# Two changes of order in a fused attention and feed-forward kernel: M's last quarter on ScalarE, and a sum on TensorE

## Chip, core and metric

The kernel runs on one core of a Trainium2 chip. The metric is the device time of one execution in microseconds (us). Engines are named as in the profile: PE is TensorE (PEld its weight loads), ACT is ScalarE, DVE is VectorE, POOL is GpSimd, and SP is SyncE, which here only issues DMAs. Each engine works through its own instructions in the order in which they were issued to it; engines wait for each other by semaphores.

## What is computed

A two-sided cross attention between tokens and a small state, and then a feed-forward product with a leaky ReLU over both results:

```python
scores = scale * x @ state.T            # x: (8, 8, 512, 64), state: (8, 8, 32, 64)
a = softmax(scores)                     # over the 32 state rows
xread = a @ state
a2 = softmax(scale * state @ x.T)       # over the 512 tokens
sread = a2 @ x
x = concat([xread, sread]) as (8 * 544, 512)
h = x @ w_in                            # (512, 2048)
out = maximum(0.01 * h, h) @ w_out      # (2048, 512)
```

Inputs and output are float32; the products run in bfloat16 with float32 sums.

## The kernel before

**Tiling.** The work goes batch by batch (b = 0 to 7). The eight heads and 32 state rows of a batch make two groups of 128 rows, so a score tile is 128 x 2 x 512. Instead of multiplying a by state and the result by w_in, the kernel forms **M** = state times w_in once per batch (`a_m`, L364), 2 x 128 rows by 2048 columns, in four quarters of 512 columns. A quarter is 8 small matmuls into PSUM, then a copy into the SBUF tile `M` (`m_evict`, L384, or copies written out). The hidden layer is then h = M.T times aT (`ff1`, L394, the class `Quad` for batch 0), a leaky ReLU on ACT, and the second product with w_out (`piece`, and from batch 1 on the class `Batch`).

**Order.** The order of all five engines is written by hand (`tc.manual_schedule`): each engine gets its instructions in the order of the calls in the source. A call such as `a_m` issues only to PE, `m_evict(.., SCA)` only to ACT, `cast_x(.., POO)` only to POOL, and the DMA calls to the queue named in them. So a line moved in the source changes the order on an engine only against lines that use the same engine.

**PSUM.** The tiles are named by tag: "sc" and "big" are one buffer of two banks each, "ph" and "py" two buffers of one bank each. A new tile of a tag waits until the old one's last reader is done.

**Batch 0 (L911 to L938).** It is done in two halves u of 256 tokens. `scores0`, `max0`, `split0`, `spread0` put score minus maximum into PSUM; `exp0(u)` (ACT, L850) makes `e10[u]`; `sum0(u)` (PE, L861, four small matmuls `r<-ones,e`) sums it; `recip0(u)` (DVE, L869) takes the reciprocal `q`; `recip0_rows` (PE, L826, `qb<-ident,q`) spreads it over rows; `probs0(u)` (DVE, L877) multiplies into `aT`. Woven into that are M's first quarter (L923), batch 1's first quarter `pm1` (L933) and M's second quarter (L934, tile "big", copied by ACT at L938 in two halves). After it come the ff products of batch 0, eight `Quad`s of four column blocks and one half of the tokens each; the first reads M's first quarter, the second, on columns 512 to 1023, M's second.

**Batches 0, 1 and 2 (L1006 to L1047).** While PE does the second product of batch 0 in pieces (`piece`, L608), batch 1 goes through its softmax: `a_scores(a1)` writes "sc" (L216), `a_shift` (DVE, L226 to L239), `a_max2` (DVE, L288, L290), `a_exp(a1)` (ACT, L246), `a_probs(a1)` (DVE, L251 to L264, the tile `aT`), and `a_exp2(a1, g)` (ACT, L296, with a read of the accumulator each), the exponentials of the other softmax, which are the last readers of the bank "sc". Batch 1's M quarters 1 to 3 go through "ph" and are copied by ACT in two copies of 128 x 512 each (L388). For batch 2 the input `xl`, loaded by a DMA on POOL's queue (L107, issued from L911), is cast to bfloat16: four heads by ACT (L1033, one instruction of 128 x 1024, L113) and four by POOL (L1035); then SP issues the DMA transpose that makes batch 2's `xT` (L1037, L200), and after it the load of batch 3's x (L1043, L107). The pieces of L1039 and the product of M's last quarter (L1040) stand behind these casts in the source. Then PE goes on with the pieces of L1047, and opens batch 2 with `pm = a_m(a2, 0, "sc")`, which takes the bank "sc", and `ff(0)`, which reads batch 1's `aT`.

**From batch 2 on** a loop over the batches repeats one weave of ff products, second products (L679), softmax steps and casts.

Of the kernel before, what the change touches and what calls it, by code (L numbers as in the profile page):

```python
# [30 lines left out]
def kernel(  # L31
# [25 lines left out]
    VEC, SCA, POO = nc.vector.tensor_copy, nc.scalar.copy, nc.gpsimd.tensor_copy  # L57
# [54 lines left out]
    def cast_x(b, h0, h1, copy):  # L112
        copy(  # L113
            xs[b][:, :, h0:h1].rearrange("p t h d -> p h t d"),
            xl[b][:, h0:h1].rearrange("p h (t d) -> p h t d", t=NT),
        )
# [68 lines left out]
    def state_t(i):  # L185
        POO(stb[i][:], stf[i][:])
        nc.sync.dma_start_transpose(st_t[i][:], stb[i][:].rearrange("p b q -> p (b q)"))
# [11 lines left out]
    def a_xt_dma(a):  # L199
        nc.sync.dma_start_transpose(  # L200
            a.xT[:].rearrange("p t k q -> p (t k) q"),
            a.xb[:].rearrange("p t h d -> p (t h d)"),
        )

    def st_of(a, g, k):
        rows = slice(D * g, D * (g + 1))
        if a.b == 0:
            return stbd[rows, k, g ^ (k // 2), :]
        t = st1 if a.b == 1 else st_t[0][:, a.b - 2] if a.b < 4 else st_t[1][:, a.b - 4]
        return t[rows, NS * k:NS * (k + 1)]  # L210
# [153 lines left out]
    def a_m(a, c, tag):  # L364
        if a.M is None:
            a.M = mpool.tile([P, 2, DFF], BF16, name="M", tag="M")
        if tag in ("ph", "py", "phpy"):
            pm = [psum.tile([P, DM], FP32, name="pm", tag=t) for t in (tag[:2], tag[-2:])]
            at = [t[:] for t in pm]
        else:  # L370
            pm = psum.tile([P, 2, DM], FP32, name="pm", tag=tag, bufs=1)
            at = [pm[:, g, :] for g in range(2)]
        for k in range(NK):
            for g in range(2):
                v, r = (k // 2, 2 * (k % 2) + (g ^ (k // 2))) if a.b == 0 else (g, k)
                nc.tensor.matmul(  # L376
                    at[v][NS * r:NS * (r + 1)],
                    lhsT=st_of(a, g, k),
                    rhs=w_in_bf[D * g:D * (g + 1), k, DM * c:DM * (c + 1)],
                    start=True, stop=True,  # L380
                )
        return pm

    def m_evict(a, c, pm, copy):  # L384
        cols = slice(DM * c, DM * (c + 1))
        if isinstance(pm, list):
            for g in range(2):
                copy(a.M[:, g, cols], pm[g][:])  # L388
        else:
            copy(a.M[:, :, cols], pm[:])  # L390
# [211 lines left out]
    def piece(b, hT, i, jq, bank=None, copy=SCA, part=range(4)):  # L602
        if jq == 0:
            y = ys[b, i] = Y()
            y.py = psum.tile([P, DM], FP32, name="py", tag="py")[:] if bank is None else bank
        y = ys[b, i]
        for j in (4 * jq + v for v in part):
            nc.tensor.matmul(  # L608
                y.py, lhsT=hT[:, j, P * i:P * (i + 1)], rhs=w_out_bf[:, j, :],
                start=(j == 0), stop=(j == 15),  # L610
            )
        if jq == 3 and copy is not None:
            y_store(b, i, copy)

    def y_store(b, i, copy):
        tag, bufs = (f"yo{i - 2}", 1) if (b, i) in ((0, 2), (0, 3)) else ("ysb", 3)
        ysb = ypool.tile([P, DM], FP32, name="ysb", tag=tag, bufs=bufs)
        copy(ysb[:], ys[b, i].py)
        if b == B:
            for bb in range(4):  # L620
                r0 = (4 * i + bb) * SROW + S
                nc.sync.dma_start(out[r0:r0 + NS, :], ysb[NS * bb:NS * (bb + 1), :])
        else:
            nc.sync.dma_start(rows_of(b)[i], ysb[:])
# [13 lines left out]
    def weights_sum(dst, m0=0, m1=NM, eng=None):  # L638
        u, v, op = (
            (B12, B11, ALU.subtract), (B11, tw[2], ALU.subtract),  # L640
            (B22, B12, ALU.add), (tw[1], B21, ALU.add),
        )[dst]
        with nc.allow_low_precision(reason="operands of a product"):
            ms = slice(m0, m1)
            (eng or nc.vector).tensor_tensor(out=tw[dst][:, ms], in0=u[:, ms], in1=v[:, ms], op=op)
# [122 lines left out]
    a0, a1, a2 = att_of[:3]  # L768
# [88 lines left out]
    def sum0(u):  # L857
        for v in range(2):
            for q in range(2):
                n = H * v + NK * q  # L860
                nc.tensor.matmul(  # L861
                    r0[u][:, n:n + NK], lhsT=e10[u][:, q, P * v:P * (v + 1)], rhs=ones4[:],
                    start=False, stop=(v == q == 1),
                )

    def recip0(u):
        q = att.tile([P, NG], BF16, name="q0", tag="q0")
        with nc.allow_low_precision(reason="one rounding, of the finished reciprocal"):
            nc.vector.reciprocal(q[:], r0[u][:])  # L869
        return q  # L870
# [52 lines left out]
    pm = a_m(a0, 0, "big")  # L923
# [7 lines left out]
    VEC(a0.M[:, 1, :DM], pm[:, 1, :])  # L931
    probs0(0)
    pm1 = a_m(a1, 0, "sc")  # L933
    pm = a_m(a0, 1, "big")  # L934
    sum0(1)
    q = recip0(1)
    for g in range(2):
        SCA(a0.M[:, g, DM:2 * DM], pm[:, g, :])  # L938

    h0 = hpool.tile([P, 16, S], BF16, name="hT", tag="hT")  # L940
# [42 lines left out]
    for u, j, tag in (  # L983
# [7 lines left out]
        if (u, j) == (0, 8):  # L991
            pm = a_m(a0, 3, "big")
# [37 lines left out]
    weights_sum(2, 0, 4, nc.gpsimd)  # L1030
    weights_sum(1, 0, 4, nc.gpsimd)
    state_t(0)
    cast_x(2, 0, 4, SCA)  # L1033
    for h in range(NK, H):
        cast_x(2, h, h + 1, POO)  # L1035
    a_open(a2, 2)
    a_xt_dma(a2)  # L1037
    for i in (2, 3):
        piece(0, h0, i, 1)  # L1039
    m_evict(a1, 3, a_m(a1, 3, "ph"), SCA)  # L1040
    for g in range(2):
        a_exp2(a1, g)
    load_x(3, nc.sync)  # L1043
# [26 lines left out]
    pm = a_m(a2, 0, "sc")  # L1070
# [42 lines left out]
    pm = [a_m(a2, 1, "big"), a_m(a2, 2, "sc")]  # L1113
# [222 lines left out]
```

## Time and profile before

| | us |
|---|---|
| median of 3 runs | 201.9 |
| lowest, highest | 201.85, 202.06 |
| the profiled execution | 202.15 |
| its span, first to last instruction | 200.4 |
| busy: DVE | 160.4 |
| busy: ACT | 143.6 |
| busy: POOL | 55.5 |

The span lies inside the execution's time; the rest is around it. A row of the timeline gives the start in us from the span's beginning, the length of a group of like instructions in us, the engine, the source line, the operation, the tiles written and read, the shape and the count; in brackets stands how long the engine was idle before and what ended that. A row of waits gives who waited for what: us in total, times, longest. A row of the chain gives start, length and what. A DMA row of the timeline is the issue alone; "us to landing" is in the view of DMA issues.

### The profile page before, as it was taken

To read this page: it belongs to the slowest core of one execution; us is meant where nothing else is said; L and a number is where in the kernel's file an instruction comes from. 1 tells how busy PE (TensorE), PEld (TensorE's weight loads), DVE (VectorE), ACT (ScalarE), POOL (GpSimd) and SP (SyncE) were. 2 spreads that over 40 slices of the span, in tenths; PEclk is the share of its full clock that TensorE was granted. 3 is DMA by queue.
4 is the path that set the end of the run, shared out by engine and by line. 5 is a ranking of instruction groups with operands and counts; after the bars stand their busy time and mean duration, and the time that the engine had idled before them with its cause. 6 is when DMAs were issued, how large, how long until landed. Compare 5 with 4: busy or idle time off the path is not lost.

```text
span 200.4 us, 4995 instructions
## 1 busy us (share of the span) xinstructions
PE 194.9 (97%) x2066; PEld 134.6 (67%) x2066; DVE 160.4 (80%) x249; ACT 143.6 (72%) x263; POOL 55.5 (28%) x82
## 2 busy tenths in 40 slices
PE   7999999999999999999999999999999999999993
PEld 2566634346676767766776677666767788799882
DVE  2576689999999989975997499779978977995622
ACT  3388747599877867978697859787878768767710
POOL 8393174690036005200420040100020024004250
PEclk9999999999999999999999999999999999999999
DMA  6999997999672892559424844290025102310035
GB/s 184 229 207 261 241 294 130 225 292 202 143 192 53 248 264 50 98 206 258 96 39 169 270 55 89 105 164 0 0 108 157 29 0 87 125 56 0 0 95 170
DMA packets 39510, 28.01 MB, mean 140 GB/s; under 512 B 25344, under 2 KB 36736, under 8 KB 39488
## 3 DMA queue, kind: packets, MB, share of 16 engines
q1 hardware_dynamic: 33712, 20.35, 39.6%
q0 software_dynamic: 4944, 6.55, 16.0%
q10 hardware_dynamic: 832, 0.79, 1.4%
q8 instruction: 16, 0.26, 0.5%
q14 instruction: 6, 0.05, 0.1%
HBM read 17.30 MB, written 8.91 MB: 131 GB/s over the span
## 4 chain that ended last, share of the span: by engine, by line
PE 80%; DMA 14%; POOL 2%; ACT 2%; issue 0%; DVE 0%; POOLq 0%
PE yq L679 43%; PE ph L397 22%; DMA xl<-in_x_dram 8%; DMA w_in_bf<-in_moe_w_in_dram 5%; PE pf L475 3%; PE pm L376 3%; PE yu L679 3%; PE pl L564 2%; PE psn L342 1%; PE sc L216 1%; PE py L608 1%; PE phw L410 1%; POOL w_in_bf L126 1%; ACT e L296 1%; ACT xb L113 1%; ACT M L388 0%
## 5 line engine op out<-in xcount | busy, mean ns | idle before, releaser
L403 ACT ACTIVATE hT<-ph 128x512 bf16<-128x512 f32 x100 | 58.5, 605 | 17.8 <-PE ph L397 17.3
L397 PE MATMUL ph<-aT,M 128*128 128x512 bf16 x200 | 57.7, 379 | 0.0
L679 PEld LDWEIGHTS <-su 128*128 128x128 bf16 x480 | 45.9, 98 | 14.8 <-DVE su L668 0.8
L679 PEld LDWEIGHTS <-hT 128*128 128x128 bf16 x336 | 32.3, 98 | 14.3 <-issue 2.5
L679 PE MATMUL yq<-tw_xf,su 128*128 128x256 bf16 x224 | 31.5, 273 | 0.0
L679 PE MATMUL yq<-w_out_bf,hT 128*128 128x256 bf16 x224 | 31.0, 273 | 0.0
L113 POOL CAST xb<-xl 128x512 bf16<-128x512 f32 (+1 forms) x24 | 13.8, 614 | 48.4 <-DMA xl<-in_x_dram 48.4
L668 DVE TENSOR_TENSOR su<-hT 128x1024 bf16<-128x1024 bf16 (+1 forms) x27 | 18.9, 703 | 6.7 <-ACT hT L403 6.7
L397 PEld LDWEIGHTS <-M 128*128 128x128 bf16 x200 | 19.5, 98 | 5.7 <-issue 0.2
L751 POOL TENSOR_TENSOR yo<-sv,sv 128x512 f32<-128x512 f32 x7 | 9.2, 1310 | 41.0 <-issue 20.3
L688 ACT COPY sv<-yq 128x512 f32<-128x512 f32 x28 | 16.3, 585 | 3.0 <-PE yq L679 2.5
L679 PE MATMUL yq<-tw_x,su 128*128 128x256 bf16 x112 | 15.5, 273 | 0.0
L679 PE MATMUL yq<-w_out_bf,su 128*128 128x256 bf16 x112 | 15.3, 273 | 0.0
L691 DVE TENSOR_TENSOR yo<-yq,sv 128x512 f32<-128x512 f32 x20 | 13.6, 682 | 1.5 <-PE yq L679 1.5
L679 PE MATMUL yq<-tw_x,hT 128*128 128x256 bf16 x104 | 14.5, 273 | 0.0
L390 ACT CAST M<-pm 128x1024 bf16<-128x1024 f32 x12 | 12.2, 1019 | 0.2 <-PE pm L376 0.2
L296 ACT ACTIVATE e<-sc,mcols 128x512 bf16<-128x512 f32 x16 | 11.0, 694 | 0.6 <-DVE mcols L290 0.6
L608 PEld LDWEIGHTS <-hT 128*128 128x128 bf16 x64 | 5.8, 98 | 7.0 <-issue 1.1
L668 DVE TENSOR_TENSOR su<-su,hT 128x1024 bf16<-128x1024 bf16 x14 | 9.7, 692 | 0.5
L288 DVE TENSOR_REDUCE mcol<-sc 128x2 f32<-128x1024 f32 x8 | 9.7, 1215 | 0.0
L668 DVE TENSOR_TENSOR su<-hT,su 128x2048 bf16<-128x2048 bf16 (+1 forms) x8 | 9.2, 1155 | 0.0
L226 DVE TRANSPOSE_TENSOR_REDUCE mrow<-sc 128x32 f32<-128x1024 f32 x7 | 8.7, 1242 | 0.5 <-PE sc L216 0.5
(173 smaller groups left out, 303.7 us busy)
## 6 DMA issues: line engine op xcount, KB each, us to landing
out_dram<-yo SPq DMA_DIRECT2D x12, 512.0 KB, 2.8
xl<-in_x_dram SPq DMA_DIRECT2D x5, 1024.0 KB, 6.7
w_in_bf<-in_moe_w_in_dram POOLq DMA_DIRECT2D x4, 512.0 KB, 7.8
w_out_bf<-in_moe_w_out_dram POOLq DMA_DIRECT2D x2, 512.0 KB, 12.6
x<-in_x_dram POOLq DMA_DIRECT2D x2, 512.0 KB, 11.5
w_out_bf<-in_moe_w_out_dram POOLq DMA_DIRECT2D x4, 256.0 KB, 13.7
xl<-in_x_dram POOLq DMA_DIRECT2D x1, 1024.0 KB, 16.6
out_dram<-ysb SPq DMA_DIRECT2D x4, 256.0 KB, 5.6
```

Of the source, the lines that this page charges most:

```text
L113: copy(xs[b][:, :, h0:h1].rearrange("p t h d -> p h t d"), xl[b][:, h0:h1].rearrange("p h (t d) -> p h t d", t=NT),)
L226: nc.vector.tensor_reduce(out=m1[:], in_=flat.rearrange("p (c j) -> p c j", j=NS), axis=AX.X, op=ALU.max, apply_transpose=True,)
L288: nc.vector.tensor_reduce(out=m2[:], in_=a.sc[:], axis=AX.X, op=ALU.max, negate=True)
L296: nc.scalar.activation(out=a.e2[:, g], in_=a.sc[:, g, :], func=AF.Exp, bias=a.m2s[:, g:g + 1], scale=SCALE, accum_out=a.r2[:, g:g + 1],)
L390: copy(a.M[:, :, cols], pm[:])
L397: nc.tensor.matmul(ph[:], lhsT=a.M[:, g, P * j:P * (j + 1)], rhs=a.aT[:, g, :], start=(g == 0), stop=(g == 1),)
L403: nc.scalar.activation(out=hT[:, j, :], in_=ph[:], func=AF.Prelu, alpha=0.01)
L668: (eng or nc.vector).tensor_tensor(out=S[n][:, ms], in0=u[:, ms], in1=v[:, ms], op=op)
L679: nc.tensor.matmul(bank[:, i, :], lhsT=lhs[:, m, P * i:P * (i + 1)], rhs=rhs[:, m, :], start=(first and m == 0 and (i == 0 or of is not No ...
L688: copy(t[:], bank)
L691: nc.vector.tensor_tensor(out=dst, in0=bank, in1=self.sv[n][:], op=ALU.add)
L751: nc.gpsimd.tensor_tensor(out=self.yo(1)[:, :, HC:], in0=f.sv[7][:], in1=f.sv[5][:], op=ALU.add)
```

## The change

Two blocks of source lines are moved. Nothing is added or removed.

In batch 0, M's second quarter is issued to PE after the second half's sums in place of ahead of them. (`recip0`, between them now, uses DVE.) In the stretch of batches 0 to 2, the second pieces of rows 2 and 3, and the product and the copies of batch 1's last M quarter, come ahead of batch 2's casts and of the DMA transpose of its x.

```diff
@@ -931,9 +931,9 @@
     VEC(a0.M[:, 1, :DM], pm[:, 1, :])
     probs0(0)
     pm1 = a_m(a1, 0, "sc")
-    pm = a_m(a0, 1, "big")
     sum0(1)
     q = recip0(1)
+    pm = a_m(a0, 1, "big")
     for g in range(2):
         SCA(a0.M[:, g, DM:2 * DM], pm[:, g, :])
 
@@ -1030,14 +1030,14 @@
     weights_sum(2, 0, 4, nc.gpsimd)
     weights_sum(1, 0, 4, nc.gpsimd)
     state_t(0)
+    for i in (2, 3):
+        piece(0, h0, i, 1)
+    m_evict(a1, 3, a_m(a1, 3, "ph"), SCA)
     cast_x(2, 0, 4, SCA)
     for h in range(NK, H):
         cast_x(2, h, h + 1, POO)
     a_open(a2, 2)
     a_xt_dma(a2)
-    for i in (2, 3):
-        piece(0, h0, i, 1)
-    m_evict(a1, 3, a_m(a1, 3, "ph"), SCA)
     for g in range(2):
         a_exp2(a1, g)
     load_x(3, nc.sync)
```

## The prediction

> **What bounds the kernel now.** I read the page first, for the busiest engine and for its clock.
>
> ```profile
> PE 194.9 (97%) x2066; PEld 134.6 (67%) x2066; DVE 160.4 (80%) x249; ACT 143.6 (72%) x263; POOL 55.5 (28%) x82
> ...
> PEclk9999999999999999999999999999999999999999
> ```
>
> TensorE (PE) is busy for 97% of the span and its granted clock is full throughout: time can only come out of PE's holes. So the next views are PE's waits from 12 us to 160 us, and the chain of waits from 28 us to 39 us.
>
> ```profile
> PE pm L376 <- ACT e L296: 0.3, 1, 0.3
> ```
>
> ```profile
> 15.66 16.56 DMA xl<-in_x_dram
> ```
>
> In 148 us PE waits noticeably once: for batch 1's column exponentials on ScalarE (ACT), which read the score bank "sc" that batch 2's first M quarter is to overwrite. The chain goes from there over ACT's copies and cast back to the one line shown, the load of batch 2's x: issued at 15.66, landed at 32.22. The timeline of ACT around it:
>
> ```profile
> 30.26 1.06 ACT L246 ACTIVATE e<-sh 128x1024 bf16<-128x1024 f32 x1 [0.37 <-DVE sh L239]
> 32.24 1.04 ACT L113 CAST xb<-xl 128x1024 bf16<-128x1024 f32 x1 [0.93 <-DMA xl<-in_x_dram]
> 33.20 1.06 ACT L388 CAST M<-pm 128x512 bf16<-128x512 f32 x2
> 34.15 0.70 ACT L296 ACTIVATE e<-sc,mcols 128x512 bf16<-128x512 f32 x1
> 34.73 0.21 ACT L296 ACTIVATION_READ_ACCUMULATOR e<-sc,mcols 128x1 f32 x1
> 34.82 0.69 ACT L296 ACTIVATE e<-sc,mcols 128x512 bf16<-128x512 f32 x1
> 35.39 0.22 ACT L296 ACTIVATION_READ_ACCUMULATOR e<-sc,mcols 128x1 f32 x1
> ```
>
> ACT stands still for 0.93 us before the cast, waiting for a load, and the copies of M's last quarter (L388) queue behind that cast. PE at the same time:
>
> ```profile
> 28.69 1.90 PE L608 MATMUL pyw<-w_out_bf,hT 128*128 128x512 bf16 x8
> 30.52 0.41 PE L376 MATMUL pm<-w_in_bf,st 64*32 64x512 bf16 x8
> ...
> 32.60 2.75 PE L608 MATMUL pyw<-w_out_bf,hT 128*128 128x512 bf16 x12
> 35.66 0.41 PE L376 MATMUL pm<-w_in_bf,st_t 64*32 64x512 bf16 x8 [0.31 <-ACT e L296]
> ```
>
> Ends of matmuls are modelled, so I count by starts. Eight matmuls of 512 columns take 1.90 and twelve 2.75, so one more costs 0.85/4 = 0.2125. The last of the twelve starts at 32.60 + 11 x 0.2125 = 34.94. An M product follows the last start by 0.34 (28.69 + 7 x 0.2125 = 30.18, then 30.52). PE could begin at 35.28 and begins at 35.66: the hole is **0.38 us**.
>
> **Edit 1: M's last quarter is copied ahead of the cast.** It adds and removes nothing. In source order the two pieces, the M product and its copies pass ACT's cast, four GpSimd (POOL) casts and the transposing DMA on SP's queue. PE's own order stays, POOL and SP issue what they issued in the same order; only ACT's order changes. The product of the last quarter (30.52, done by 30.93) is ready in time, so the two copies now run in the 0.93 us gap: they need about 33.20 to 34.15 = 0.95, starting at ACT's end of the exponential, some 0.95 after its start at 30.26 (a 1024-column cast frees ACT after 33.20 - 32.24 = 0.96). So copies 31.2 to 32.2, then the cast at about 32.24 as before, then the exponentials at 33.20 in place of 34.15. Their end goes from 35.61 to **34.66**, 0.6 ahead of the 35.28 at which PE wants the bank. (With the 0.22 of edit 2 below all of it is later by that: 34.9, still ahead.) The hole of 0.38 goes, no more, since PE's own pieces come late next. Queued behind the two copies on ACT is the cast, for which SP's transpose of batch 2 waits; other conditions of these 0.38 are:
>
> ```profile
> st_t<-stb SPq DMA_TRANSPOSE x1, 3.8
> ```
>
> ```profile
> 31.16 1.74 SPq L187 DMA_TRANSPOSE st_t<-stb  x1
> ```
>
> ```profile
> 32.27 1.43 POOL L113 CAST xb<-xl 128x256 bf16<-128x256 f32 x4 [1.15 <-DMA xl<-in_x_dram]
> ```
>
> ```profile
> 34.76 0.69 DVE L264 TENSOR_TENSOR aT<-e,qb 128x1024 bf16<-128x1024 bf16 x1
> ```
>
> The transposed states land at 31.16 + 3.8 = 34.96, before 35.28. The transpose of x waits for POOL's casts (32.27 + 1.43 = 33.70) as much as for ACT's (33.28): ACT may slip 0.4 before it tells. VectorE's (DVE) aT ends at 35.45; the first ff product, 0.34 after an M product (15.96 to 16.30 below), needs it at 35.62. Without these covers edit 1 would be worth less, down to nothing. Price: **-0.38**, bounds -0.38 to 0.
>
> **Edit 2: second sums ahead of M's second quarter.** PE, and what ACT and DVE do with it:
>
> ```profile
> 12.12 0.40 PE L376 MATMUL pm<-w_in_bf,stbd 64*32 64x512 bf16 x8
> 12.45 0.25 PE L861 MATMUL r<-ones,e 128*128 128x4 bf16 x4
> 12.76 0.60 PE L958 MATMUL ph<-aT,M 128*128 128x256 bf16 x4
> 13.28 0.41 PE L826 MATMUL qb<-ident,q 128*32 128x128 bf16 x16
> 13.62 1.54 PE L958 MATMUL ph<-aT,M 128*128 128x256 bf16 x12
> 14.99 1.04 PE L958 MATMUL php<-aT,M 128*128 128x256 bf16 x8
> 15.96 0.41 PE L376 MATMUL pm<-w_in_bf,stbd 64*32 64x512 bf16 x8
> 16.30 0.39 PE L958 MATMUL ph<-aT,M 128*128 128x256 bf16 x2
> ```
>
> ```profile
> 10.09 0.25 PE L855 MATMUL r<-eps,ident 128*128 128x16 bf16 x4
> 10.27 0.41 PE L376 MATMUL pm<-w_in_bf,stbd 64*32 64x512 bf16 x8
> ```
>
> ```profile
> 11.79 0.60 ACT L850 ACTIVATE e<-scn 128x512 bf16<-128x512 f32 x1 [0.46 <-PE scn L826]
> 12.59 1.07 ACT L938 CAST M<-pm 128x512 bf16<-128x512 f32 x2 [0.20 <-PE pm L376]
> ```
>
> ```profile
> 12.02 0.69 DVE L877 TENSOR_TENSOR aT<-e,qb 128x512 bf16<-128x512 bf16 x1
> 12.74 0.26 DVE L869 RECIPROCAL q<-r 128x16 bf16<-128x16 f32 x1
> 13.82 0.69 DVE L877 TENSOR_TENSOR aT<-e,qb 128x512 bf16<-128x512 bf16 x1 [0.82 <-PE qb L826]
> ```
>
> The sums read e, which ACT ends at 11.79 + 0.60 = 12.39, so they cannot start before about 12.45, where they start now. The M product filled exactly this wait (12.12 to 12.45). Put behind the sums it leaves the wait empty. It then starts 0.18 to 0.19 after them (10.09 to 10.27), at 12.64, and the ff product 0.34 after that (15.96 to 16.30), at 12.98 in place of 12.76: **+0.22** on PE. Nothing comes sooner in return: the reciprocal starts at 12.74 right behind DVE's 12.02 + 0.69 = 12.71, and its use at 13.28 is set by PE's order. ACT's two copies wait 0.47 for their product (12.12 to 12.59), so they run 13.11 to 14.18 in place of 12.59 to 13.66, 0.52 late. Queued behind them are the leaky ReLUs; and PE waits for them with its third to sixth product pair, at 13.62 + 4 x 0.11 = 14.06, its weights 0.11 sooner: 13.95 becomes 14.17, and 14.18 plus a hand-over of 0.04 is some 0.05 late. The group of twelve lasts 1.54 where 1.04 + 4 x 0.11 = 1.48 would do (eight take 1.04, four 0.60, so one more 0.11): it holds a wait of 0.06, for the aT of 13.82, which takes that up. So +0.22 again; if ACT's 0.52 came through whole, +0.52. Does a later wait swallow it? By the view of waits PE has none until 35.66, so the 0.22 travels there. Alone, edit 2 would vanish in the hole of 0.38; once edit 1 closes the hole, it counts. Bounds 0 to +0.52, taken +0.22, as the rows of the same pairs of products say.
>
> **Sum.** -0.38 + 0.22 = **-0.16**. On the profiled execution, 202.15 with a span of 200.4 and 1.75 around it, that gives 202.0; the median of the runs shown is 0.25 lower, 201.9, and 201.9 - 0.16, rounded, is **201.75**.
>
> **The rivals.** *The loss is hidden after all* (edit 2 at 0): 201.9 - 0.38 = 201.52. For it speaks only that PE has some small waits of its own; against it, that each shown start after 12.45 follows from the one before.
>
> *The timed runs have no such hole.* The profiled execution is 0.25 above their median. If the x load lands 0.3 or more sooner without a profiler, edit 1 finds nearly nothing, and edit 2 has its price: 201.9 - 0.08 + 0.22 = 202.04, **slower**. It decides from a landing 0.15 sooner than 32.22. For it: the hole hangs on one DMA of 16.56 us; against it: three runs lie within 0.21 us.
>
> *A late transpose takes the wait's place.* DVE is shifted 0.22 too, since its chain starts at batch 1's scores. POOL's weight sums start as DVE's end, then come batch 3's casts and its transpose:
>
> ```profile
> 36.93 2.12 POOL L645 TENSOR_TENSOR tw_x<-tw_xf,w_out_bf 128x1024 bf16<-128x1024 bf16 x1 [3.22 <-DVE tw_xf L645]
> ```
>
> ```profile
> 45.47 2.65 SPq L200 DMA_TRANSPOSE xT<-xb  x1
> ```
>
> ```profile
> xT<-xb SPq DMA_TRANSPOSE x1, 6.0
> ```
>
> ```profile
> 51.94 0.11 PEld L216 LDWEIGHTS <-st_t 64*32 64x32 bf16 x8 [0.42 <-issue]
> ```
>
> It lands at 45.47 + 6.0 = 51.47, PE wants it at 51.94: 0.47 spare, of which 0.16 + 0.22 go. From a further 0.1 it decides. A landing late by 0.8 costs 0.7: 201.75 + 0.7 = 202.45, slower. For it: 6.0 against 3.8 for the smaller transpose shows crowded queues; against it: 0.1 is still left.
>
> [...]
>
> **Chances.** Forecast 50%; no hole in the timed runs 18%; loss hidden 14%; late transpose 13%; clock 1%; something larger and faster 4%. About 0.2% (0.4 us) is what a measurement can tell: faster needs less than 201.5, slower more than 202.3. From the forecast and the no-hole case nearly all is "same", a good half of the hidden-loss case and the unknown faster one give faster (with a tail of the forecast), the transpose, the clock and the upper tails give slower: faster 0.20, same 0.59, slower 0.21. The likeliest case alone spans 201.55 to 202.0. The range takes in the full -0.38 and +0.52 less a little of each tail: 201.45 to 202.35.
>
> **What would show it.** Right: ACT's L388 copies of the last quarter end before the L113 cast; exponentials end near 34.9 (30.26's chain shifts by 0.22); PE's wait for ACT e L296 is gone; PE's second M product at 12.64 and the ff product at 12.98; the M product of batch 2 at about 35.5. Wrong: the ff product still at 12.76; a wait at 35.6 on another engine or a landing; a PE hole at 51.9; or equal starts at 35.7 with another end, which would put the cause later than I looked.

## The result and the profile after

The changed kernel takes 201.55 us (median of 12 runs, 201.32 to 201.72), the kernel before beside it 201.96 (12 runs, 201.73 to 202.44): a ratio of 0.9976, 95% interval 0.9969 to 0.9984. That is 0.41 us faster by the medians and 0.48 by the ratio (its interval is 0.32 to 0.63), where 0.16 was forecast. The profiled execution took 201.57 with a span of 199.8.

First the page's chain of work that ended last, by engine, before and after:

```profile
PE 80%; DMA 14%; POOL 2%; ACT 2%; issue 0%; DVE 0%; POOLq 0%
```

```profile
PE 96%; DVE 1%; issue 1%; ACT 1%
```

The load of batch 2's x, which with one load of w_in held the 14% of this chain before, is gone from it: the chain is nearly all PE's own work. Next ScalarE's timeline from 30 us to 37 us (start, length, engine, line, operation):

```profile
30.00 1.06 ACT L246 ACTIVATE e<-sh 128x1024 bf16<-128x1024 f32 x1 [0.37 <-DVE sh L239]
30.96 1.05 ACT L388 CAST M<-pm 128x512 bf16<-128x512 f32 x2
31.91 1.06 ACT L113 CAST xb<-xl 128x1024 bf16<-128x1024 f32 x1
32.85 0.70 ACT L296 ACTIVATE e<-sc,mcols 128x512 bf16<-128x512 f32 x1
33.44 0.21 ACT L296 ACTIVATION_READ_ACCUMULATOR e<-sc,mcols 128x1 f32 x1
33.53 0.69 ACT L296 ACTIVATE e<-sc,mcols 128x512 bf16<-128x512 f32 x1
34.10 0.21 ACT L296 ACTIVATION_READ_ACCUMULATOR e<-sc,mcols 128x1 f32 x1
```

The two copies fill the gap in which ACT waited for the load. In this execution the load landed at 31.84, before the copies were done, so the cast follows at once, and the exponentials end at 34.31. PE takes the bank "sc" 0.7 us later, straight behind its pieces; its timeline from 33.9 us on:

```profile
33.63 1.46 PE L608 MATMUL pyw<-w_out_bf,hT 128*128 128x512 bf16 x6
35.02 0.41 PE L376 MATMUL pm<-w_in_bf,st_t 64*32 64x512 bf16 x8
```

No idle time stands in brackets: the hole is closed. And PE at 12 us, where edit 2 works:

```profile
11.41 0.41 PE L376 MATMUL pm<-w_in_bf,st 64*32 64x512 bf16 x8
11.96 0.25 PE L861 MATMUL r<-ones,e 128*128 128x4 bf16 x4
12.14 0.41 PE L376 MATMUL pm<-w_in_bf,stbd 64*32 64x512 bf16 x8
12.48 0.61 PE L958 MATMUL ph<-aT,M 128*128 128x256 bf16 x4
```

From the first M product to the ff product it is 12.48 - 11.41 = 1.07. The first product of the same group in the profile before started at 11.89, so 12.76 - 11.89 = 0.87 there: 0.20 lost where 0.22 was forecast, by the mechanism that was forecast. Up to the M product of batch 2 it is 35.02 - 11.41 = 23.61 against 35.66 - 11.89 = 23.77: **0.16 gained, the forecast to the hundredth**. From there to the end of the span both traces take the same, 200.4 - 35.66 = 164.7 and 199.8 - 35.02 = 164.8. But the two differ by 0.6 in their spans, and what is left of that lies ahead of both edits: this execution's first M product came 0.48 sooner, at 11.41. So the hundredth is an agreement with one stretch of one trace, and not with the time. Two things are therefore open: whether this earlier start is chance, and where 0.4 us in the median come from.

### The profile page after: what moved, and what is told of

Read it like the earlier page. It is cut to its first block, busy times and chain, and to the rows that moved or that the text cites. A ratio compares the mean times of both kernels' runs of the same rounds, so it can differ in the third digit from the quotient of the medians.

```text
span 199.8 us, 4974 instructions
## 1 busy us (share of the span) xinstructions
PE 193.2 (97%) x2044; PEld 134.3 (67%) x2066; DVE 160.8 (80%) x249; ACT 143.5 (72%) x263; POOL 55.4 (28%) x82
## 4 chain that ended last, share of the span: by engine, by line
PE 96%; DVE 1%; issue 1%; ACT 1%
PE yq L679 44%; PE ph L397 20%; PE pm L376 4%; PE py L608 4%; PE pyw L608 4%; PE pf L475 3%; PE yu L679 3%; PE ph L958 3%; PE pspin L142 2%; PE pl L564 2%; PE sc L216 1%; PE psn L342 1%; PE php L958 1%; PE phw L410 1%; PE scn L826 1%
## 5 line engine op out<-in xcount | busy, mean ns | idle before, releaser
L397 PE MATMUL ph<-aT,M 128*128 128x512 bf16 x180 | 54.4, 379 | 0.3
```

Of the source, the lines that this page charges most:

```text
L397: nc.tensor.matmul(ph[:], lhsT=a.M[:, g, P * j:P * (j + 1)], rhs=a.aT[:, g, :], start=(g == 0), stop=(g == 1),)
```

## The experiments

All were timed beside runs of the kernel before on the same chip.

| kernel | median us | before beside it | ratio, 95% interval |
|---|---|---|---|
| the changed kernel | 201.55 | 201.96 | 0.9976, 0.9969 to 0.9984 |
| edit 1 alone | 201.68 | 201.99 | 0.9981, 0.9973 to 0.9990 |
| edit 2 alone | 202.08 | 201.99 | 1.0001, 0.9993 to 1.0010 |
| before, three repeats | 202.18 | 201.99 | 1.0007, 0.9999 to 1.0016 |
| changed, three repeats | 202.33 | 201.99 | 1.0017, 1.0007 to 1.0026 |
| edit 1, other weights | 201.54 | 202.06 | 0.9975, 0.9964 to 0.9986 |
| edit 1, split pieces | 201.58 | 202.06 | 0.9976, 0.9967 to 0.9986 |
| edit 1, one repeat | 201.81 | 202.06 | 0.9982, 0.9971 to 0.9992 |
| changed, split pieces | 201.66 | 202.06 | 0.9983, 0.9975 to 0.9992 |
| edit 1, no waits for two loads | 201.74 | 202.12 | 0.9982, 0.9972 to 0.9991 |
| changed, no waits for two loads | 201.67 | 202.12 | 0.9981, 0.9972 to 0.9990 |

An interval is some 0.2 us to either side, so the times alone tell apart only steps larger than that, and two changed kernels only if they differ by some 0.3; for the smaller steps the traces are read.

**Edit 1 alone.** The second hunk of the change, without the first.

> Edit 1 alone (the copies of M's last quarter ahead of the cast). The hole as read (0.38 us in the profiled execution of before): 0.38 faster than before, and 0.22 faster than the changed kernel. The larger hole (in the timed runs TensorE reaches the wait some 0.25 us sooner than in that one execution, while the load lands when it lands, so the hole is 0.63 and the sum -0.63 + 0.22 = -0.41): 0.63 faster than before, 0.22 faster than the changed kernel. The hidden loss (hole 0.38 to 0.41, edit 2 costs nothing): 0.41 faster than before, the same as the changed kernel.

Measured: 0.31 faster than before by the medians, and *not* faster than the changed kernel (201.68 against 201.55). The third account fits. The second misses both its numbers; the first has the 0.38 inside the interval (0.20 to 0.55 faster), but not the 0.22 against the changed kernel: without edit 2's loss nothing more is gained. The trace shows the loss really is absent; PE from 11.3 us on:

```profile
11.48 0.41 PE L376 MATMUL pm<-w_in_bf,st 64*32 64x512 bf16 x8
11.71 0.40 PE L376 MATMUL pm<-w_in_bf,stbd 64*32 64x512 bf16 x8
12.04 0.25 PE L861 MATMUL r<-ones,e 128*128 128x4 bf16 x4
12.35 0.60 PE L958 MATMUL ph<-aT,M 128*128 128x256 bf16 x4
```

12.35 - 11.48 = 0.87. And yet PE from 33.9 us on, with its weight loads below:

```profile
33.55 1.61 PE L608 MATMUL pyw<-w_out_bf,hT 128*128 128x512 bf16 x6
35.09 0.41 PE L376 MATMUL pm<-w_in_bf,st_t 64*32 64x512 bf16 x8
```

```profile
33.98 0.31 PEld L608 LDWEIGHTS <-hT 128*128 128x128 bf16 x2
34.57 0.10 PEld L608 LDWEIGHTS <-hT 128*128 128x128 bf16 x1 [0.28 <-issue]
```

The M product of batch 2 comes 35.09 - 11.48 = 23.61 after the first, exactly as in the changed kernel. The same six matmuls take 1.61 where they take 1.46 there, and the weight loader stands still for 0.28 ahead of the load at 34.57, where it is 0.12 between two of these loads in the changed kernel (four of 0.098 in 0.75, from 33.85 on). The piece in question is the last of row block 2, and its third matmul is the first to read the last part of w_out. The view names no releaser; the DMA that brings this part, issued at 20.72, landed at 34.52, 0.05 ahead. A smaller wait of the same kind, 0.06, stands at 24.20, for the cast of batch 1's x. Together they make 0.21 of the 0.22 that edit 2 costs. So a new account was formed: *landings*. With edit 1 alone PE comes to data of two DMAs before they are there, and edit 2's loss falls into these waits.

**Edit 2 alone.** The first hunk of the change.

> Edit 2 alone (second sums ahead of M's second quarter). The hole as read and the larger hole: within 0.05 us of before, since the 0.22 shows in the trace from 12.7 us on but ends in the wait for the exponentials, whose hole is 0.22 shorter. The hidden loss: the same time too, but with the ff product right after the sums and no shift of 0.22 in the trace.

Measured: 0.09 slower by the medians, the ratio 1.0001 with 1 well inside: no change, as all accounts had it, and with the shift in the trace (the ff product at 12.98, the first M product at 11.90, so 1.08), which the third account did not expect. It ends in the hole: PE's M product of batch 2 again at 35.67, the hole by starts 0.15 in place of 0.38.

**Repeats ahead of the hole.**

```diff
-    def a_m(a, c, tag):
+    def a_m(a, c, tag, extra=0):
...
-        for k in range(NK):
+        for k in [*range(NK)] * (1 + extra):
...
-    m_evict(a1, 3, a_m(a1, 3, "ph"), SCA)
+    m_evict(a1, 3, a_m(a1, 3, "ph", 3), SCA)
```

> The kernel before, with the eight matmuls of batch 1's last M quarter issued four times instead of once (the same values written again): some 3 x 0.22 = 0.66 us more work on TensorE ahead of the hole, nothing else. The hole as read, and the hidden loss: 0.66 - 0.38 = 0.28 slower than before. The larger hole: 0.66 - 0.63, at most 0.05 slower.

> The changed kernel with the same three repeats. All theories in which the hole is closed: 0.66 slower than the changed kernel (some 0.25 slower than before), which measures the price of the repeats themselves.

Measured: the kernel before gets 0.19 slower (0.14 by the ratio), the changed one 0.78 (0.66 expected). Both traces show 0.65 of work added, so by the times some 0.5 of it went into the hole in the first. That lies between the 0.38 that was read and the 0.63 of the second account, and the interval of the first (-0.02 to +0.32 us) holds 0.28 as well as 0.05: the times do not settle the size.

The two traces say more. These are PE's first M product of batch 1 and that of batch 2, of the kernel before with repeats and then of the changed kernel with repeats:

```profile
11.82 0.41 PE L376 MATMUL pm<-w_in_bf,st 64*32 64x512 bf16 x8
...
35.86 0.41 PE L376 MATMUL pm<-w_in_bf,st_t 64*32 64x512 bf16 x8
```

```profile
11.89 0.41 PE L376 MATMUL pm<-w_in_bf,st 64*32 64x512 bf16 x8
...
36.15 0.41 PE L376 MATMUL pm<-w_in_bf,st_t 64*32 64x512 bf16 x8
```

It is 24.04 in the first: 0.27 more than the 23.77 of the kernel before, for 0.65 of work, so 0.38 went into the hole, as it was read. And it is 24.26 in the second, 0.22 more than in the first. Both executions started late, like the profile that the prediction was made from, and neither waits on the way (24.04 - 0.65 is 23.39, the length in the trace with other weights below, where the waits are gone). There edit 2 costs its full price.

**The wait for w_out taken away, in two ways.** Both start from edit 1 alone. In the first the piece reads other weights:

```diff
-                y.py, lhsT=hT[:, j, P * i:P * (i + 1)], rhs=w_out_bf[:, j, :],
+                y.py, lhsT=hT[:, j, P * i:P * (i + 1)],
+                rhs=w_out_bf[:, j - 4 * ((b, i, jq) == (0, 2, 3)), :],
```

> Edit 1 alone, and the last piece of row block 2 of batch 0 reads the third quarter of w_out in place of the fourth, so that TensorE has no load to wait for there (this part of the output is then another product). The landings theory (with the hole closed and without edit 2, TensorE comes 0.22 us sooner to loads that land when they land: in the trace of edit 1 alone it waits 0.16 at 34.57 us for the last part of w_out and 0.06 at 24.20 for batch 1's x; edit 2's loss of 0.22 falls into these two waits and costs nothing): 0.16 faster than edit 1 alone, 0.16 faster than the changed kernel. The rival (edit 2 costs nothing because its 0.22 is given back on TensorE elsewhere): the same time as edit 1 alone.

In the second two matmuls of the next piece are put ahead:

```diff
-    piece(0, h0, 2, 3, copy=None)
+    for i, part in ((2, (0, 1)), (3, (0, 1)), (2, (2, 3))):
+        piece(0, h0, i, 3, copy=None, part=part)
...
-    piece(0, h0, 3, 3, copy=None)
+    piece(0, h0, 3, 3, copy=None, part=(2, 3))
```

> Edit 1 alone, with the last pieces of row blocks 2 and 3 of batch 0 interleaved: two matmuls of block 3 that need only what landed at 33.2 us stand ahead of the two of block 2 that need the last part of w_out, so that the latter start 0.43 later; nothing is left out. The landings theory: 0.16 faster than edit 1 alone, as with the other weights, and 0.1 to 0.2 faster than the changed kernel, the best of all. The rival: the same as edit 1 alone.

Measured: 201.54 and 201.58, that is 0.14 and 0.10 below edit 1 alone where 0.16 was expected. Against the runs of before beside them they stand at 0.9975 and 0.9976 where edit 1 alone stands at 0.9981. Both go the landings account's way, within an uncertainty larger than the step. In the trace with other weights the wait is gone (M product of batch 2 at 34.95, the first at 11.56: 23.39, or 0.22 less than with edit 1 alone). But neither time is below that of the changed kernel, where 0.16 and 0.1 to 0.2 were expected: here the landings account misses, or the times are too coarse for it.

**A loss of edit 2's size elsewhere.** Edit 1 alone, with one repeat of the M product in place of three (the diff above with 1).

> Edit 1 alone, with the eight matmuls of batch 1's last M quarter issued twice (0.22 us more on TensorE at 30.2 us, a loss of the size of edit 2's, at another place). The landings theory: 0.16 of it falls into the wait for w_out, so at most 0.06 slower than edit 1 alone. The rival: 0.22 slower than edit 1 alone.

Measured: 201.81, 0.13 above edit 1 alone, midway between the two accounts. In its trace the waits lay elsewhere: PE waited 0.23 and 0.09 for the casts of batch 1's x at 22.95 and 24.36, ahead of the repeat. Inconclusive.

**The split pieces on the changed kernel.**

> The changed kernel with the same interleaved pieces. The landings theory: it has no wait for w_out to lose, so the same time as the changed kernel within 0.05 us. The rival: the same as well; but a gain of 0.16 here would mean that the interleaving helps by itself, and not by the wait.

Measured: 201.66 against 201.55, no gain, as both accounts had it: interleaving by itself doesn't help.

**Both waits taken away, with and without edit 2.** Beside the other weights, batch 1 is cast from batch 0's x:

```diff
-            x1[u][:].rearrange("p h (t d) -> p h t d", t=NT),
+            xf[u][:].rearrange("p h (t d) -> p h t d", t=NT),
```

> Edit 1 alone, with two waits for loads taken away: batch 1 is cast from batch 0's x, which has long landed, in place of its own, and the last piece of row block 2 of batch 0 reads w_out's third quarter in place of the fourth (these parts of the output are other products). Landings theory: 0.2 us faster than edit 1 alone and 0.2 faster than the next kernel, since edit 2's loss has no wait left to fall into; up to 0.1 of that may go into the landing of the transposed states at 34.8. The rival (edit 2's loss is given back elsewhere on TensorE): the same time as the next kernel.

> The changed kernel with the same two waits for loads taken away. Landings theory: within 0.1 us of the changed kernel, and 0.1 to 0.2 slower than the kernel ahead of it in this call, whose only difference is the place of the second sums; in the trace the M product of batch 2 follows the ff product of batch 0 as closely in both (some 22.5 us), and the 0.22 ahead of the ff product stays to the end. The rival: the same time as the kernel ahead of it.

Measured: 201.74 and 201.67, no difference, as the rival had it; the landings account had 0.1 to 0.2. Below stand PE's waits from 12 us to 160 us in the kernel without edit 2 (the one with edit 2 has none), and then the weight loads at 35 us, without edit 2 first and with it second:

```profile
PE sc L216 <- DMA xT<-xb: 0.4, 1, 0.4
PE pm L376 <- DMA st_t<-stb: 0.2, 1, 0.2
```

```profile
35.13 0.11 PEld L376 LDWEIGHTS <-st_t 64*32 64x32 bf16 x8 [0.68 <-DMA st_t<-stb]
```

```profile
35.10 0.11 PEld L376 LDWEIGHTS <-st_t 64*32 64x32 bf16 x8 [0.50 <-DMA st_t<-stb]
```

Behind the two loads stands a third landing, of the transposed states, at 35.09 and 35.06 here, and both kernels wait for it, the one without edit 2 by 0.18 longer. (In the twelve other traces the loader is idle there for 0.42.) Edit 2's loss was there up to this point: the second transposes start 12.66 us after the first M product without edit 2 and 12.89 with it. At the M product of batch 2 it is 23.64 and 23.69: the next landing has taken the loss. The other wait of the first kernel, 0.4 for the transpose of batch 2's x (issued at 33.84, landed 4.8 us later, where the median of the six such transposes is 4.3 in the traces of before and of the changed kernel), comes behind that and makes its profiled execution 202.13, against 201.66. So the times alone fit the rival as well; it is the traces that speak for landings.

**The kernel before, profiled twice more.**

> The kernel before once more, for a second profile. The larger hole: where TensorE starts batch 1's first M product sooner than at 11.89 us (11.4 to 11.5 in the traces of the changed kernel and of edit 1 alone), the hole at the M product of batch 2 is 0.5 to 0.8 us, and the time stays within 0.2 of 202. The hole as read: 0.38 whatever the start.

> The same, a third profile: hole and start move against each other, the sum stays. The hole as read: 0.38 whatever the start.

One time each, 202.30 and 202.37. The starts came sooner, 11.40 and 11.48, and this is the third profile's PE, first its wait, then its rows from 22.8 us on; the changed kernel's rows for the same stretch stand below.

```profile
PE pm L376 <- ACT e L296: 0.4, 1, 0.4
```

```profile
22.61 0.38 PE L608 MATMUL py<-w_out_bf,hT 128*128 128x512 bf16 x1
22.94 0.62 PE L1014 MATMUL pxt<-ident,xb 128*128 128x128 bf16 x8
23.40 1.03 PE L608 MATMUL pyw<-w_out_bf,hT 128*128 128x512 bf16 x4
24.37 0.62 PE L1014 MATMUL pxt<-ident,xb 128*128 128x128 bf16 x8
```

```profile
22.55 0.59 PE L608 MATMUL py<-w_out_bf,hT 128*128 128x512 bf16 x2
22.98 0.61 PE L1014 MATMUL pxt<-ident,xb 128*128 128x128 bf16 x8
23.43 1.03 PE L608 MATMUL pyw<-w_out_bf,hT 128*128 128x512 bf16 x4
24.29 0.61 PE L1014 MATMUL pxt<-ident,xb 128*128 128x128 bf16 x8
```

In the third profile the second transposes start 24.37 - 23.40 = 0.97 after the piece, in the changed kernel 0.86: 0.11 of waiting. The first transposes start 0.33 after the last matmul ahead of them, in the changed kernel 0.22 (22.98 less 22.55 less one matmul of 0.21): another 0.11. What they wait for is VectorE's cast of batch 1's x, and that waits for its DMA (this profile's DVE):

```profile
22.19 0.69 DVE L999 CAST xb<-x 128x1024 bf16<-128x1024 f32 x1 [0.96 <-DMA x<-in_x_dram]
23.62 0.69 DVE L999 CAST xb<-x 128x1024 bf16<-128x1024 f32 x1 [0.73 <-DMA x<-in_x_dram]
```

In the first profile the same casts came just in time. Its DVE, then its PEld, at the end of which stands the weight load of the first matmul that needs the last part of w_out:

```profile
22.18 0.69 DVE L999 CAST xb<-x 128x1024 bf16<-128x1024 f32 x1 [0.73 <-DMA x<-in_x_dram]
23.59 0.69 DVE L999 CAST xb<-x 128x1024 bf16<-128x1024 f32 x1 [0.72 <-DMA x<-in_x_dram]
```

```profile
23.03 0.65 PEld L1014 LDWEIGHTS <-xb 128*128 128x128 bf16 x8
...
24.34 0.65 PEld L1014 LDWEIGHTS <-xb 128*128 128x128 bf16 x8
...
34.76 0.10 PEld L608 LDWEIGHTS <-hT 128*128 128x128 bf16 x1
```

The casts end at 22.87 and 24.28, 0.16 and 0.06 ahead of the transposes, and this part of w_out landed at 34.62, 0.14 ahead of its use. Nobody waits, and nobody has more than that to spare.

And the third profile from 33.9 us on:

```profile
33.72 1.59 PE L608 MATMUL pyw<-w_out_bf,hT 128*128 128x512 bf16 x6
35.68 0.41 PE L376 MATMUL pm<-w_in_bf,st_t 64*32 64x512 bf16 x8 [0.37 <-ACT e L296]
```

0.13 more for w_out (1.59 against 1.46), and a hole of 0.06 more than in the first profile (0.37 idle against 0.31), so 0.44. From the first M product to that of batch 2 it is 35.68 - 11.48 = 24.20, 0.43 more than in the first profile of before, though the kernel is the same: a start that is 0.41 sooner is lost in four waits, for two halves of x, for w_out and for the exponentials, and the M product of batch 2 stays where the load of batch 2's x puts it (35.66, 35.73 and 35.68 in the three profiles, by landings at 32.22, 32.29 and 32.24). The hole did grow, but to 0.44 in both early profiles and not to the 0.5 to 0.8 of the larger hole; the rest of the earlier start is lost before it.

## Why the prediction came out as it did

- *The bound, and edit 1's mechanism: right.* PE is the bound (busy for 97% of the span in both pages), its only large wait was the one for the exponentials behind cast and copies, and it is gone. ACT's order came as worked out, and the exponentials end at 34.31 in the changed kernel and 34.49 with edit 1 alone, ahead of PE; the 34.9 was forecast for a late start, and the one late trace with edit 1 has the repeats in it (35.23). The transpose on SP follows POOL's casts as before: they end at 31.89 + 1.44 = 33.33 in the changed kernel, and it is issued at 33.35 (33.70 and 33.73 before).
- *The size of the hole: nearly right.* 0.38 in the profile that was read and by the repeats, 0.44 in two more.
- *Edit 2's price on the spot: right.* From the first M product to the ff product 0.86 or 0.87 (0.94 in the second profile of before) becomes 1.07 or 1.08 in each trace with edit 2, and nothing came sooner in return.
- *What became of that price: wrong.* The step that failed reads: "By the view of waits PE has none until 35.66, so the 0.22 travels there." In the one profile that was read, PE was late, and the casts of batch 1's x and the last part of w_out were ready only 0.06 to 0.16 us ahead of it, which the view of waits doesn't show, since nobody waited. In an early execution PE can come to them before they are ready (it waited 0.16 and 0.06 with edit 1 alone, 0.11, 0.11 and 0.13 in the third profile of before), and a loss ahead of them is then taken from the wait. The term of +0.22 holds for a late execution (24.26 against 24.04 with the repeats). As a term for the timed runs it was mis-sized: it measures about 0 there (edit 1 alone 201.68, both edits 201.55, some 0.3 uncertain), and in the two early traces both kernels take 23.61 us from the first M product to batch 2's. Without it the sum is the hole alone, -0.38 to -0.44, near the measured -0.41.
- *The time: in part luck.* 201.55 lies inside the range of 201.45 to 202.35 because the range was wide, and at the edge of the likeliest case (201.55 to 202.0). The gain is 0.41 where the sum gave 0.16.
- *The rivals.* The one that gave 201.52, the loss hidden after all, is what the timed runs fit: PE did have small waits of its own, but they belong to landings, and these traces show them (0.06 to 0.23 for x and w_out) only after early starts. The case of no hole in the timed runs, with edit 1 worth 0.08, is ruled out by edit 1 alone (0.20 to 0.55 faster). Yet the three profiled executions of before (202.15, 202.30 and 202.37) are all above the medians of its timed runs, 201.9 to 202.12, and no run here shows why. The late transpose of batch 3 cost nothing in the changed kernel's trace: it landed at 51.12, 0.18 ahead of its use at 51.30. A transpose that came late was seen once, in the run without waits for loads, that of batch 2's x (4.8 us to landing, PE's wait 0.4). A lower clock, to which the chances give 1%, was not seen in the changed kernel: its page has 9 in all 40 slices, those behind the hole from 11.41 + 0.41 to 11.96 too, and its timed runs were granted 0.997 to 1.0. That hole is 0.14; the 0.33 from 12.12 to 12.45 runs from the start of the product that had filled it.
- *Still open:* how the timed runs divide between early and late starts, since only profiled executions show the start; so how much of the 0.41 is hole and how much is the start that the kernel now keeps. The two early profiles of before and that of the changed kernel don't settle it: between them the M product of batch 2 comes 0.66 to 0.71 sooner (35.68 and 35.73 against 35.02), but the load of batch 2's x also landed 0.40 to 0.45 sooner in the latter. Ten of fourteen traces have the first M product at 11.37 to 11.56 us, four at 11.82 to 11.90.

## What to carry to other kernels

A loss on the bound engine costs its full time only if no wait stands between it and the end (here 0.22 after late starts and about 0 after early ones), and a view of waits shows only the waits of that execution: list also what was ready just ahead of its use (here 0.06 to 0.16), for that is the next wait when the engine comes sooner. A gain is capped in the same way: here three landings stand close to PE's need (the casts of x 0.06 to 0.16 us ahead in one trace, waited for by 0.06 to 0.23 in others; w_out 0.14 ahead, and 0.13 to 0.16; the transposed states 0.32 ahead, and 0.19), and with two of the waits taken away the third took 0.18 of edit 2's 0.23. And one profile gives one start: where a load is in the chain, take two or three profiles of the same kernel before reading a hole of 0.4 us as its size (here 0.38, 0.44 and 0.44 after starts at 11.89, 11.40 and 11.48).

## What was not expected of the hardware

The same program starts in two ways. VectorE's casts of batch 0's x, in the first profile of before and in the third:

```profile
6.08 1.12 DVE L120 CAST xb<-xf 128x256 bf16<-128x256 f32 x5 [1.05 <-DMA xf<-in_x_dram]
```

```profile
5.53 1.35 DVE L120 CAST xb<-xf 128x256 bf16<-128x256 f32 x5 [0.48 <-DMA xf<-in_x_dram]
```

The wait for the first loads is 1.05 us in one and 0.48 in the other, and the first M product of batch 1 follows at 11.89 and 11.48. The load of batch 2's x, issued ten microseconds later, lands at 32.22 and 32.24 all the same. Over the fourteen traces it lands at 31.84 to 32.33 after the ten early starts and at 32.01 to 32.27 after the four late ones: an early start of the engines didn't bring an early landing.
